# Attention and mixture kernel: values read once, POOL residues, a third turning bank and a new order

## The chip, the cores and the metric

The program runs on one core of a Trainium2 chip. The time is in device microseconds (us), the median of several executions of the whole program. The core's engines are TensorE (PE, with its weight load PEld), VectorE (DVE), ScalarE (ACT), GpSimd (POOL) and SyncE (SP). Each engine goes through its own instructions in a fixed order; semaphores hold an instruction back until what it needs is there. DMAs are issued from the queues of SP, ACT and POOL.

## The reference

Three layers, in float32, for 4 batches of 576 tokens. Attention with 8 heads of 64 and a decay; a gated mixture of 4 attention experts with top-2 routing; and a mixer: a low-rank mix over the sequence and a ReLU layer of 2048.

```python
scores = q @ k.T / 8 + cum[:, None] - cum[None, :]        # cum = cumsum(log(clip(f)))
x = softmax(where(causal, -1e9, scores)) @ v              # 8 heads -> x[B, 576, 512]
for e in range(4):                                        # mixture: q, k, v of x per expert
    ye = softmax(causal(x@wq[e] @ (x@wk[e]).T / 8)) @ (x@wv[e]) @ wo[e]
    out += gate_top2[e] * ye
u = out + (out.T @ U @ V).T                               # mixer; U, V, w_ch1, w_ch2 are float64
return u + maximum(u @ w_ch1, 0) @ w_ch2
```

## The kernel before

Most products are taken in pairs of float16: a number is scaled by a power of two, its rounded part `hi` is written by ACT and the rest, `lo = scale * x - hi`, by DVE (`split`); three products of hi and lo then give nearly float32. The scale comes from a largest or summed absolute value of the whole tile (`pow2`, with one small PE product `mm<-identr,cols` that spreads it over the partitions, and `scales`).

The work is written as generators ("threads"). A planner (`Plan`) runs them in simulated time: each thread says which engine it needs next, or which buffer of a ring (`Ring`) or event, and the planner picks the thread with the earliest time plus a penalty by its priority (`PR`, times `PEN`). The order in which it picks is the order in which the instructions stand on each engine. `LAG` is the time that it adds before a freed buffer may be taken again, and `BIAS` what it adds for an engine where a step may go to one of several (`Any`). None of these numbers stands in the program itself; they only move instructions and choose engines.

By batch the stages are these. Kind 1 is the attention of 8 heads: `scores` (PE, into the PSUM ring `sp`, 3 banks, or `acc`), `softmax` (DVE mask and maximum, ACT exp), the turning of the probabilities, and `pair_pv` with `pv_out` (the product with the values, in ring `mm`, 2 banks, and its division). `project` and `values_gates` form the experts' q, k, v and the gates. Kind 2 is the experts' attention, by the same functions. `mix` forms z; `hidden` (tiles `hid<-z,wfr`, ring `hid`, 1 bank) and `outputs` (tiles `acc<-w2x,g` and `acc<-wo,z`) are the last two layers, with `relu` between them. After `mix` of a batch its hidden and output products fill PE beside the heads of the next batch.

Probabilities are turned in one of two ways. For batch 0, and for the first two heads of batch 1, PE turns the float32 blocks (`turn_head`, line 628, `mm<-identr,sc`) and the split reads them from PSUM (`pt<-mm`). Elsewhere the split is taken first (tiles P, by `parts`: its second half on DVE or POOL) and a DMA turns P into pt.

Batch 0 carries extra work beside its heads: the weights w1 and w2 come as float64 and are turned to float32 (`f64_to_f32`: ACT, DVE and, for one product, POOL; tiles x, w2x, sg), w1 is folded with wo on PE (`fold`, ring `hid`, tiles `hid<-x,wtr`, into wfr), and wfr, w2x, wall, wo and U are split. `hidden` waits for all splits of wfr (`ev("wf")`) and for z.

`values` reads each batch's values v in four pieces of two heads (tile vr, 2 buffers, 320 KB each): once for the sum of the absolute values, and a second time, when the common scale SV is known, for the split into V (tiles V, 2 buffers of hi and of lo).

Of the kernel before, what the change touches and what calls it, by code (L numbers as in the profile page):

```python
# [20 lines left out]
KB = 5  # L21
# [3 lines left out]
EPS = 1e-9 * 2.0 ** 14  # L25
BIAS = {'act': 100.0, 'dve': 900.0, 'pool': 0.0}
XN = 1
# [13 lines left out]
WARM = 3300.0  # L41
LAG = 200.0
AHEAD = 16
PROJ_EXP = 15
PR = {'load': 4.25, 'low0': 1.25, 'low': 6.0, 'zeros': 1.75, 'scores': 1.5, 'soft0': 1, 'soft2_0': 2.0, 'soft': 6.5, 'soft2_': 6.5, 'pv0': -2.0, 'pv': 3.25, 'pvout0': 0, 'pvout': 3.25, 'project0': 3.5, 'project': 3.25, 'vg0': -1.25, 'vg': 4.25, 'out0': 1.0, 'out': 5.0, 'values0': 0.75, 'values': -0.75, 'wall': 4.5, 'prep': 5.0, 'f64': 0.5, 'f64_2': 2.25, 'fold': 1.75, 'wf': 0.5, 'w2': 6.25, 'mix': 0.0, 'relu': 1.5, 'store': -0.25, 'hidden': 4.5, 'outputs': 6}
TERMS = ((0, 0), (0, 1), (1, 0))

NEXT = (2, 0, 0, 0)
HEADS = [(1, 0, h) for h in range(8)]
ON_PE = lambda kind, b, h: b == 0 or (kind, b) == (1, 1) and h < NEXT[0]  # L50
for b_, n_ in enumerate(NEXT):
# [84 lines left out]


class Plan:
    GAP = {"pe": 0.0, "act": 130.0, "dve": 115.0, "pool": 130.0, "sp": 0.0}
# [49 lines left out]
    def run(self):  # L189
        while self.threads:  # L190
# [32 lines left out]
def attn_moe_mixer(ctx: ExitStack, tc: tile.TileContext, qk, v, f, wall, wot, wo, w1, w2, u3, v3, out):  # L223
# [213 lines left out]

    HY = {}
    HG, PT, VP, XT, SV, STG, GATE, YT, YN, IV, ZT, CS = {}, {}, {}, {}, {}, {}, {}, {}, {}, {}, {}, {}
# [106 lines left out]
    def softmax(key, blk, st, early, both):  # L546
# [5 lines left out]
        hold = key if blk else (kind, b, h // 2)  # L552
        on_pe = ON_PE(*key)
        if blk == 0 and on_pe:
# [58 lines left out]
    def turn_head(key):  # L613
# [5 lines left out]
        for c, blks, k0, k1 in ((0, (0, 1), 0, 5), (3, (2,), 0, 5), (6, (3,), 0, 5), (10, (4,), 0, 4), (14, (4,), 4, 5)):  # L619
            for blk in blks:  # L620
                yield ev("exp", key, blk)
            bank = yield r_mm
            i = 0
            for blk in blks:
                x = EXP[key, blk]
                yield "pe"
                for kb in range(k0, min(k1, blk + 1)):
                    nc.tensor.transpose(bank[:, 128 * i:128 * i + 128], x[:, 128 * kb:128 * kb + 128], identr)  # L628
                    plan.tensor(110, 128)
# [3 lines left out]

            def out_(bank=bank, c=c, i=i):
                hi, lo = (pt[:, 15 * t + c:15 * t + c + i, :].rearrange("k c q -> k (c q)") for t in range(2))
                yield from split(hi, lo, bank[:, :128 * i], 2.0 ** 14)
                r_mm.free(bank)
                n.done()
# [27 lines left out]
    def pair_pv(kind, b, p):  # L666
# [4 lines left out]
        else:  # L671
            yield ev("v2", b)
            vs, c0 = V2, 2 * p
        on_pe = ON_PE(kind, b, 2 * p)
        if not on_pe:
# [3 lines left out]
        for j in range(2):  # L679
# [33 lines left out]
    def pv_out(kind, b, p, j, bank, pv):  # L713
# [7 lines left out]
        yield "dve"  # L721
        ts(rr, pv[:, :, 64], EPS, ALU.add)
        recip(rr, rr)
# [39 lines left out]
    def values(b):  # L763
        if True:
            mx = col(f"mxv{b}", 4)
            for hp in range(4):
                vr = yield r_vr
                if hp == 2:
                    yield ev("rows of first")
                yield QUEUE[3]  # L770
                got = dma(vr, v[b][:, :, hp * 128:(hp + 1) * 128], queue(3))
                yield got
                yield "act"
                abssum(mx[:, hp:hp + 1], vr, vr)
                r_vr.free(vr)
            e = yield from pow2(f"v{b}", mx, 4)
            SV[b] = scales(f"v{b}", e, 14)
            for hp in range(4):
                vr = yield r_vr
                hi = yield r_vp[0]  # L780
                lo = yield r_vp[1]
                VP[b, hp] = (hi, lo)
                yield QUEUE[3]
# [3 lines left out]
                yield from split(hi[:, :, :, 0:64], lo[:, :, :, 0:64], x, SV[b][0])  # L787
                r_vr.free(vr)
                ev("vp", b, hp).done()
            if b + 1 < B:  # L790
                spawn(values(b + 1), PR['values'])

# [632 lines left out]
```

## Time and profile before

| | |
|---|---|
| median of 3 runs | 787.75 us (783.74 to 790.79) |
| the profiled execution: time, span | 790.84 us, 789.1 us |
| busy: PE, DVE, ACT, POOL | 667.4, 491.9, 425.9, 278.6 us |
| TensorE clock granted, mean | 0.942 |
| DMA | 110.64 MB, mean 140 GB/s |

The page and the views say for each engine how long it worked and what ended the idle time ahead of its instructions. Busy times of engines overlap, so they don't add up to the span. A granted clock of 1.00 is TensorE's 2.4 GHz, and 0.50 its lower level of 1.2 GHz; a stretch in between had both. In the rows, L241 is `mm`, L246 `act`, L252 `dve`, L264 `pool`, L270 and L272 the DMAs.

### The profile page before, as it was taken

The page shows a single profiled execution, that of the slowest core. Times are in us where ns is not written, and L with a number is a line of the kernel's source. Part 1 is how long each engine was busy: PE and PEld are TensorE (multiplying, and loading weights), DVE is VectorE, ACT ScalarE, POOL GpSimd, SP SyncE. Part 2 cuts the span into 40 slices and gives each one's busy share as a digit, 9 for nine tenths or more (in the row PEclk, how much of TensorE's full clock was granted, in tenths as well). Part 3 has the DMA queues.
Part 4 walks back from the last instruction along what each step waited for, and adds up shares of the span by engine and source line. Part 5 has one row for each costly group of instructions (what it writes and reads, how often), then busy time and mean ns, then how long its engine had stood idle before and what let it go on. Part 6 is the DMA issues. An engine that isn't in the chain of part 4 may idle for free.

```text
span 789.1 us, 15849 instructions
## 1 busy us (share of the span) xinstructions
PE 667.4 (85%) x5802; PEld 465.6 (59%) x5802; DVE 491.9 (62%) x1551; ACT 425.9 (54%) x891; POOL 278.6 (35%) x341
## 2 busy tenths in 40 slices
PE   2768897877578889898699898994999999899996
PEld 1456787655555557565466575663666756555553
DVE  4898797999979744775766366866663673311111
ACT  3777886787857643664557355654553562211121
POOL 4123235306745420477664114773751241000000
PEclk9999999977769999999799999996999999899999
DMA  8556545647899964999999549999985675000000
GB/s 232 162 133 178 158 128 155 202 116 180 173 179 153 149 152 100 184 193 228 210 187 181 107 120 184 183 211 203 184 145 93 121 133 80 27 0 27 1 27 27
DMA packets 213730, 110.64 MB, mean 140 GB/s; under 512 B 165012, under 2 KB 194708, under 8 KB 213620
## 3 DMA queue, kind: packets, MB, share of 16 engines
q1 hardware_dynamic: 182740, 79.37, 51.0%
q0 software_dynamic: 8096, 16.22, 10.7%
q10 hardware_dynamic: 22816, 14.03, 6.8%
q8 instruction: 46, 0.75, 0.4%
q14 instruction: 32, 0.26, 0.1%
HBM read 57.15 MB, written 5.16 MB: 79 GB/s over the span
## 4 chain that ended last, share of the span: by engine, by line
PE 33%; DMA 13%; DVE 9%; ACT 4%; issue 2%; POOL 1%; SPq 0%; ACTq 0%; DVEq 0%; POOLq 0%
PE acc L241 12%; PE mm L241 12%; DMA pt<-P 8%; PE hid L241 8%; DVE sc L252 2%; DVE P L252 2%; PE sp L241 2%; DMA R<-in_qk 2%; DMA PT<-P 1%; ACT P L246 1%; ACT sc L246 1%; DVE rr L252 1%; DMA wq<-lg 1%; DVE nm L252 1%; POOL P L264 1%
## 5 line engine op out<-in xcount | busy, mean ns | idle before, releaser
L241 PE MATMUL acc<-w2x,g 128*128 128x512 f16 x768 | 183.1, 384 | 0.4 <-DVE g L252 0.4
L264 POOL TENSOR_TENSOR P<-sc,P 128x320 f16<-128x320 f32 (+4 forms) x111 | 86.6, 787 | 171.1 <-ACT P L246 145.4
L241 PEld LDWEIGHTS <-g 128*128 128x128 f16 x864 | 82.5, 99 | 85.5 <-issue 3.0
L241 PE MATMUL hid<-z,wfr 128*128 128x256 f16 x864 | 115.6, 284 | 10.2 <-DVE g L252 5.9
L246 ACT ACTIVATE sc<-sc,nm 128x192 f32<-128x192 f32 (+4 forms) x185 | 99.8, 555 | 45.4 <-DVE nm L252 41.6
L252 DVE SCALAR_TENSOR_TENSOR g<-hid,g 128x512 f16<-128x512 f32 x72 | 49.5, 687 | 111.4 <-ACT g L246 111.1
L241 PEld LDWEIGHTS <-wfr 128*128 128x128 f16 x864 | 85.4, 102 | 36.6 <-issue 10.5
L246 ACT ACTIVATE g<-hid 128x512 f16<-128x512 f32 x72 | 42.5, 591 | 98.6 <-PE acc L241 62.0
L246 ACT ACTIVATE P<-sc 64x64 f16<-64x64 f32 (+4 forms) x163 | 69.4, 458 | 38.9 <-DMA pt<-P 35.7
L241 PE MATMUL mm<-V,pt 128*128 128x65 f16 x2058 | 76.3, 198 | 11.7 <-DMA pt<-P 5.3
L241 PEld LDWEIGHTS <-pt 128*128 128x128 f16 x2058 | 71.6, 101 | 14.9 <-issue 6.7
L241 PE MATMUL sp<-X 128*128 128x256 f32 (+1 forms) x132 | 51.9, 402 | 27.3 <-DVE nm L252 14.0
L252 DVE TENSOR_TENSOR P<-sc,P 128x576 f16<-128x576 f32 (+4 forms) x59 | 47.7, 811 | 35.7 <-ACT P L246 32.9
L264 POOL TENSOR_TENSOR xh<-xn,xh 128x320 f16<-128x320 f32 x30 | 26.8, 892 | 82.9 <-ACT xh L246 80.0
L628 PE MATMUL mm<-identr,sc 128*128 128x128 f32 x210 | 38.5, 302 | 17.8 <-DVE pt L252 12.4
L241 PEld LDWEIGHTS sp<-X 128*128 128x128 f32 x132 | 27.5, 208 | 40.0 <-DVE nm L252 20.4
L241 PE MATMUL mm<-xt,wall 128*128 128x288 f16 x384 | 49.6, 286 | 1.1 <-DVE stg L252 0.5
L252 DVE CUSTOM_DVE_ANT_0 sc<-sp,mask 64x64 f32<-64x64 f32 (+4 forms) x110 | 46.1, 424 | 6.5 <-PE sp L241 4.1
L264 POOL TENSOR_TENSOR x<-x,sg 128x512 f32<-128x512 f32 (+2 forms) x19 | 25.8, 1355 | 54.8 <-DVE x L252 42.8
L241 PEld LDWEIGHTS <-wall 128*128 128x128 f16 x384 | 37.5, 98 | 11.7 <-issue 1.9
L628 PEld LDWEIGHTS mm<-identr,sc 128*128 128x128 f32 x210 | 25.7, 151 | 31.6 <-DVE pt L252 15.0
L241 PE MATMUL sp<-Y 68*128 68x256 f32 (+1 forms) x132 | 42.4, 329 | 0.0
(142 smaller groups left out, 1194.8 us busy)
## 6 DMA issues: line engine op xcount, KB each, us to landing
wd<-in_w SPq DMA_DIRECT2D x32, 512.0 KB
vr<-in_v ACTq DMA_DIRECT2D x32, 320.0 KB
R<-in_qk SPq DMA_DIRECT2D x22, 288.0 KB
Y<-in_qk POOLq DMA_DIRECT2D x22, 288.0 KB, 4.7
X<-in_qk POOLq DMA_DIRECT2D x22, 288.0 KB, 5.6
out_dram<-o SPq DMA_DIRECT2D x18, 256.0 KB
Xh<-stg SPq DMA_DIRECT2D x16, 216.0 KB
X<-in_qk POOLq DMA_DIRECT2D x22, 144.0 KB, 4.7
```

What stands on the lines that cost most here:

```text
L241: nc.tensor.matmul(out_, lhsT=lhsT, rhs=rhs, start=start, stop=stop, **kw)
L246: nc.scalar.activation(out_, in_, fn, **kw)
L252: getattr(nc.vector, op)(**kw)
L264: getattr(nc.gpsimd, op)(out=out_, **kw)
L628: nc.tensor.transpose(bank[:, 128 * i:128 * i + 128], x[:, 128 * kb:128 * kb + 128], identr)
```

## The change

- `values` reads each piece once. Scales are taken by half a batch (two pieces): both pieces are loaded, summed (into a scratch tile `junk` from ring `xn`), scaled by their half's own scale and split from the same tile. When the second half's scale is known, a common scale SV is formed and a factor for each half (`RV`), which `pv_out` multiplies into the row sums. `pair_pv` of kind 1 waits for that (`ev("sv", b)`).
- `split` of a tile in SBUF may take its residue to POOL alone: two POOL operations (the scaling in place, then the subtraction) in place of one on DVE.
- `turn_head` of batch 0 takes a bank of `mm` or the bank of `hid`, whichever the planner has free earlier (`Either`).
- Which pairs PE turns stands in a table `TURN`. It names the same pairs as the expression before.
- `LAG` is 100 in place of 200, the bias of DVE 1000 in place of 900, and nearly all priorities `PR` are others.

```diff
-BIAS = {'act': 100.0, 'dve': 900.0, 'pool': 0.0}
+BIAS = {'act': 100.0, 'dve': 1000.0, 'pool': 0.0}
-LAG = 200.0
+LAG = 100.0
-PR = {'load': 4.25, 'low0': 1.25, 'low': 6.0, 'zeros': 1.75, 'scores': 1.5, 'soft0': 1, ...
+PR = {'load': 2.75, 'low0': -1.5, 'low': 6.0, 'zeros': -2.0, 'scores': 3.25, 'soft0': 1, ...
+TURN = {(1, 0): 4, (2, 0): 2, (1, 1): 1, (1, 2): 0}
+class Either:
+    def ready(self):
+        return any(r.ready() for r in self.rings)
+    def take(self, *a):
+        r = min((r for r in self.rings if r.ready()), key=lambda r: r.time())
+        return r, r.take(r.shape, r.dtype, r.name)
...
     def split(hi, lo, src, scale=1.0):
         yield "act"
         copy_scaled(hi, src, scale)
-        yield "dve"
-        residue(lo, src, hi, scale)
+        n = size(src)
+        if src.space == PSUM or (yield Any(dve=170 + 1.04 * n, pool=2 * (180 + 1.93 * n))) == "dve":
+            if src.space == PSUM:
+                yield "dve"
+            residue(lo, src, hi, scale)
+        else:
+            pool("tensor_scalar", src, in0=src, scalar1=scale, scalar2=None, op0=ALU.mult)
+            yield "pool"
+            pool("tensor_tensor", lo, in0=src, in1=hi, op=ALU.subtract)
...
-            bank = yield r_mm
+            r, bank = yield Either(*((r_mm, r_hid) if key[1] == 0 else (r_mm,)))
...
+            if kind == 1:
+                yield ev("sv", b)
...
-        ts(rr, pv[:, :, 64], EPS, ALU.add)
+        if kind == 1:
+            ts(rr, pv[:, :, 64], EPS, ALU.add, RV[b][p // 2], ALU.mult)
+        else:
+            ts(rr, pv[:, :, 64], EPS, ALU.add)
...
     def values(b):
...
+        for half in range(2):
+            for i in range(2):
                 vr = yield r_vr
...
+                got = dma(vr, v[b][:, :, hp * 128:(hp + 1) * 128], queue(3))
+            for i, (vr, got) in enumerate(vrs):
                 yield got
+                junk = yield r_xn.of([128, KB, 128], F16, "junk")
                 yield "act"
-                abssum(mx[:, hp:hp + 1], vr, vr)
-                r_vr.free(vr)
+                abssum(mx[:, i:i + 1], vr, junk)
+                r_xn.free(junk)
+            e = yield from pow2(f"v{b}{half}", mx, 2)
+            ss.append(scales(f"v{b}{half}", e, 14)[0])
+            if half == 1:
+                tt(e, es[0], es[1], ALU.max)
+                SV[b] = scales(f"v{b}", e, 14)
+                RV[b] = [times(f"rv{b}{i}", s, SV[b][1]) for i, s in enumerate(ss)]
+                ev("sv", b).done()
...
-                got = dma(vr, v[b][:, :, hp * 128:(hp + 1) * 128], queue(3))
-                yield got
...
+                yield from split(hi[:, :, :, 0:64], lo[:, :, :, 0:64], x, ss[half])
```

How the instructions then stand is shown at three places. Counted over the whole program, POOL takes over residues of two parts of wall and of two rows of wfr, and 16 P subtractions; DVE has 44 small instructions on `cols` more and 16 P subtractions fewer; ACT issues 16 reads of vr fewer; 95 of the 210 turning products go to the bank of `hid`.

**ACT at the program's start.** YW are the tiles of the first heads' q and k, aug the decay rows, vr the values, V their split. Before:

```order
L246 ACTIVATE vr,cols<-vr 128x640
L272 DMA vr<-in_v 128x5x128
L246 ACTIVATE vr,cols<-vr 128x640
L272 DMA YW_96<-aug 4x2x576
L272 DMA YW_94<-aug 4x2x576
L272 DMA vr<-in_v 128x5x128
L272 DMA YW_95<-in_qk 64x2x576
L272 DMA YW_95<-aug 4x2x576
L246 ACT_TABLE_LOAD
L246 ACTIVATE sc_97<-sp,nm 64x64
```

And now:

```order
L267 ACTIVATE junk,cols<-vr 128x640 x2
L293 DMA YW_96<-aug 4x2x576
L293 DMA YW_94<-aug 4x2x576
L267 ACTIVATE V_78<-vr,cols 128x10x64
L293 DMA YW_95<-in_qk 64x2x576
L293 DMA YW_95<-aug 4x2x576
L267 ACTIVATE V_79<-vr,cols 128x10x64
L267 ACT_TABLE_LOAD
L267 ACTIVATE sc_97<-sp,nm 64x64
L267 ACTIVATE sc_98<-sp,nm 128x192
L293 DMA vr<-in_v 128x5x128 x2
```

The first two pieces of the values are split ahead of the first exponential, and the third head's load now stands behind the first of these splits.

**PE at the first heads.** `sp` and `acc` are scores, `identr,sc` turned blocks, with the bank that they go to ahead of the arrow. Before:

```order
L241 MATMUL sp<-YW_96 128x64
L241 MATMUL sp<-YW_96 128x192
L241 MATMUL sp<-YW_96 128x320
L628 MATMUL mm<-identr,sc_97 128x128
L628 MATMUL mm<-identr,sc_98 128x128 x2
L241 MATMUL sp<-YW_96 128x448
L628 MATMUL mm<-identr,sc_99 128x128 x3
L241 MATMUL acc<-YW_96 128x288 x2
L241 MATMUL sp<-YW_94 128x64
L628 MATMUL mm<-identr,sc_100 128x128 x4
```

And now:

```order
L262 MATMUL sp<-YW_96 128x64
L262 MATMUL sp<-YW_96 128x192
L262 MATMUL sp<-YW_96 128x320
L262 MATMUL sp<-YW_96 128x448
L658 MATMUL hid<-identr,sc_97 128x128
L658 MATMUL hid<-identr,sc_98 128x128 x2
L262 MATMUL acc<-YW_96 128x288
L658 MATMUL mm<-identr,sc_99 128x128 x3
L262 MATMUL acc<-YW_96 128x288
L658 MATMUL mm<-identr,sc_100 128x128 x4
```

Turned blocks alternate over three banks, and a score product stands between them more often.

**POOL late in batch 0.** X, Y and R are the heads of batch 1 (X is the residue that their scores need), P the probabilities' residues, wfr the folded weights that `hidden` waits for. Before, with all eight residues of wfr on DVE, ahead of z:

```order
L264 TENSOR_TENSOR P_74<-sc_98,P_74 128x192
L272 DMA Y<-in_qk 64x2x576
L264 TENSOR_TENSOR X<-R,Y 64x576
L272 DMA X<-in_qk 64x2x576
L264 TENSOR_TENSOR X<-R,X 64x576
L264 TENSOR_TENSOR P_75<-sc_101,P_75 128x576
L272 DMA X<-in_qk 64x576
L264 TENSOR_TENSOR xh<-xn,xh 128x5x64
L264 TENSOR_TENSOR P_73<-sc_97,P_73 64x64
L264 TENSOR_TENSOR X<-R,Y 64x576
```

And now:

```order
L285 TENSOR_SCALAR wfr<-wfr,cols 128x512
L293 DMA Y<-in_qk 64x2x576
L285 TENSOR_TENSOR wfr<-wfr 128x512
L293 DMA X<-in_qk 64x2x576
L285 TENSOR_TENSOR P_75<-sc_100,P_75 128x448
L293 DMA X<-in_qk 64x576
L285 TENSOR_TENSOR P_75<-sc_101,P_75 128x576
L285 TENSOR_TENSOR X<-R,Y 64x576
L285 TENSOR_SCALAR wfr<-wfr,cols 128x512
L293 DMA Y<-in_qk 64x2x576
L285 TENSOR_TENSOR wfr<-wfr 128x512
```

The second residue of wfr on POOL now stands behind the residue X of the fourth head of batch 1 that is loaded this way, and on DVE four of the six that are left stand behind z's.

## Rows read from the trace of the kernel before

**Rows 1.** Busy time by stage: from:to, length, busy (instructions) by engine, PEclk, DMA share, GB/s.

```profile
20.00:232.00 212.00, 161.91 (x1531) 129.34 (x1530) 186.84 (x536) 160.60 (x343) 75.42 (x69) 0.91 0.65 162
232.00:276.00 44.00, 37.09 (x333) 25.44 (x331) 37.30 (x103) 30.52 (x61) 22.21 (x25) 0.95 0.93 143
276.00:680.00 404.00, 361.57 (x3333) 248.03 (x3332) 242.53 (x872) 210.13 (x448) 172.57 (x211) 0.95 0.85 158
680.00:789.20 109.20, 102.33 (x603) 59.64 (x601) 16.59 (x24) 18.34 (x30) 0.00 (x0) 0.97 0.04 15
```

**Rows 2.** DVE's waits, 20 to 232 us: total us, times, longest us.

```profile
DVE pt L252 <- ACT pt L246: 4.9, 8, 1.0
DVE rr L252 <- PE mm L241: 4.5, 7, 1.5
```

**Rows 3.** The chain that ended last, by engine.

```profile
PE 33%; DMA 13%; DVE 9%; ACT 4%; issue 2%; POOL 1%; SPq 0%; ACTq 0%; DVEq 0%; POOLq 0%
```

**Rows 4.** PE's waits, 232 to 680 us.

```profile
PE mm L241 <- DMA PT<-P: 8.6, 3, 3.4
...
PE sp L241 <- POOL X L264: 5.1, 1, 5.1
```

**Rows 5.** The chain in order of time, where the tail begins.

```profile
677.99 9.52 PE hid L241 x59
```

**Rows 6.** DVE in order of time: start, us, what, idle before.

```profile
17.08 0.24 DVE L252 CUSTOM_DVE_ANT_0 sp<-sp,mask 64x64 f32<-64x64 f32 x1 [6.36 <-PE sp L241]
```

**Rows 7.** DVE's groups by shape, 0 to 276 us: busy us, mean ns.

```profile
L252 DVE SCALAR_TENSOR_TENSOR V<-vr,cols,V 128x640 f16<-128x640 f32 x8 | 8.4, 1049 | 0.7 <-ACT V L246 0.6
...
L252 DVE SCALAR_TENSOR_TENSOR wfr<-wfr,cols 128x512 f16<-128x512 f32 x8 | 6.0, 747 | 0.0
...
L252 DVE SCALAR_TENSOR_TENSOR wall<-w2x,cols,wall 128x1024 f16<-128x1024 f32 x3 | 4.8, 1584 | 0.0
...
L252 DVE TENSOR_TENSOR cols<-cols 128x1 f32<-128x1 f32 x11 | 3.6, 330 | 0.3
...
L252 DVE TENSOR_SCALAR cols<-cols 128x1 f32<-128x1 f32 x24 | 3.6, 151 | 0.7
...
L252 DVE TENSOR_TENSOR P<-sc,P 128x320 f16<-128x320 f32 x5 | 2.8, 550 | 0.0
...
L252 DVE TENSOR_TENSOR P<-sc,P 128x448 f16<-128x448 f32 x2 | 1.9, 936 | 0.0
```

**Rows 8.** PE's waits, 0 to 232 us.

```profile
PE mm L628 <- DVE pt L252: 12.4, 15, 2.3
```

**Rows 9.** DMA on the page: all bytes, and two kinds of issues.

```profile
DMA packets 213730, 110.64 MB, mean 140 GB/s; under 512 B 165012, under 2 KB 194708, under 8 KB 213620
...
vr<-in_v ACTq DMA_DIRECT2D x32, 320.0 KB
...
Y<-in_qk POOLq DMA_DIRECT2D x22, 288.0 KB, 4.7
```

**Rows 10.** POOL's group of the float64 products, 0 to 290 us.

```profile
L264 POOL TENSOR_TENSOR x<-x,sg 128x512 f32<-128x512 f32 x16 | 23.0, 1436 | 29.7 <-DVE x L252 17.6 <-PE mm L628 5.8 <-ACT sc L246 3.2
```

**Rows 11.** POOL and DVE in order of time, 249 to 258.6 us.

```profile
251.37 1.40 POOL L264 TENSOR_TENSOR X<-R,X 64x576 fp32r<-64x576 f32 x1
251.41 1.92 DVE L252 SCALAR_TENSOR_TENSOR w2x<-w2x,cols 128x512 f16<-128x512 f32 x1
...
254.11 0.75 DVE L252 SCALAR_TENSOR_TENSOR w2x<-w2x,cols 128x512 f16<-128x512 f32 x1 [0.32 <-ACT w2x L246]
```

**Rows 12.** The hidden stage's start, in order of time, 228 to 240 us.

```profile
232.26 1.38 PE L241 MATMUL hid<-z,wfr 128*128 128x256 f16 x6
...
236.00 1.40 POOL L264 TENSOR_TENSOR X<-R,Y 64x576 fp32r<-64x576 f32 x1
```

**Rows 13.** The next such residue of X on POOL.

```profile
248.80 1.39 POOL L264 TENSOR_TENSOR X<-R,Y 64x576 fp32r<-64x576 f32 x1 [0.90 <-DMA R<-in_qk]
```

**Rows 14.** Busy time, 220 to 240 us.

```profile
220.00:240.00 20.00, 17.10 (x129) 12.32 (x129) 16.42 (x52) 11.85 (x22) 11.11 (x12) 0.66 0.87 167
```

More of the change, by code (lines that the diff above doesn't have):

```diff
@@ L41 @@
 WARM = 3300.0
-LAG = 200.0
+LAG = 100.0
 AHEAD = 16
 PROJ_EXP = 15
-PR = {'load': 4.25, 'low0': 1.25, 'low': 6.0, 'zeros': 1.75, 'scores': 1.5, 'soft0': 1, 'soft2_0': 2.0, 'soft': 6.5, 'soft2_': 6.5, 'pv0': -2.0, 'pv': 3.25, 'pvout0': 0, 'pvout': 3.25, 'project0': 3.5, 'project': 3.25, 'vg0': -1.25, 'vg': 4.25, 'out0': 1.0, 'out': 5.0, 'values0': 0.75, 'values': -0.75, 'wall': 4.5, 'prep': 5.0, 'f64': 0.5, 'f64_2': 2.25, 'fold': 1.75, 'wf': 0.5, 'w2': 6.25, 'mix': 0.0, 'relu': 1.5, 'store': -0.25, 'hidden': 4.5, 'outputs': 6}
+PR = {'load': 2.75, 'low0': -1.5, 'low': 6.0, 'zeros': -2.0, 'scores': 3.25, 'soft0': 1, 'soft2_0': 1.0, 'soft': 5.5, 'soft2_': 7.0, 'pv0': -1.0, 'pv': 1.75, 'pvout0': 2.0, 'pvout': 4.75, 'project0': 3.75, 'project': 2.25, 'vg0': 0.75, 'vg': 4.75, 'out0': 1.0, 'out': 3.0, 'values0': 1.0, 'values': -1.0, 'wall': 5.25, 'prep': 6.5, 'f64': -1.25, 'f64_2': 3.25, 'fold': 2.25, 'wf': 1.75, 'w2': 3.75, 'mix': 0.25, 'relu': 0.0, 'store': 2.75, 'hidden': 6.25, 'outputs': 8.25}
 TERMS = ((0, 0), (0, 1), (1, 0))
+TURN = {(1, 0): 4, (2, 0): 2, (1, 1): 1, (1, 2): 0}
 NEXT = (2, 0, 0, 0)
 HEADS = [(1, 0, h) for h in range(8)]
-ON_PE = lambda kind, b, h: b == 0 or (kind, b) == (1, 1) and h < NEXT[0]
 for b_, n_ in enumerate(NEXT):
@@ L135, in free, with __init__, of, time @@
             self.over.done(self.end[id(t)])
+class Either:
+    def __init__(self, *rings):
+        self.rings = rings
+    def of(self, shape, dtype, name):
+        return self, shape, dtype, name
+    def ready(self):
+        return any(r.ready() for r in self.rings)
+    def time(self):
+        return min(r.time() for r in self.rings if r.ready())
+    def take(self, *a):
+        r = min((r for r in self.rings if r.ready()), key=lambda r: r.time())
+        return r, r.take(r.shape, r.dtype, r.name)
 class Plan:
@@ L552, in softmax @@
         hold = key if blk else (kind, b, h // 2)
-        on_pe = ON_PE(*key)
+        on_pe = key[2] // 2 < TURN.get(key[:2], 0)
         if blk == 0 and on_pe:
@@ L632, in turn_head, with out_ @@
                     r_sc[blk].free(EXP.pop((key, blk)))
-            def out_(bank=bank, c=c, i=i):
+            def out_(r=r, bank=bank, flat=flat, c=c, i=i):
                 hi, lo = (pt[:, 15 * t + c:15 * t + c + i, :].rearrange("k c q -> k (c q)") for t in range(2))
-                yield from split(hi, lo, bank[:, :128 * i], 2.0 ** 14)
-                r_mm.free(bank)
+                yield from split(hi, lo, flat[:, :128 * i], 2.0 ** 14)
+                r.free(bank)
                 n.done()
@@ L673, in pair_pv @@
             vs, c0 = V2, 2 * p
-        on_pe = ON_PE(kind, b, 2 * p)
+        on_pe = p < TURN.get((kind, b), 0)
         if not on_pe:
@@ L763, in values @@
     def values(b):
-        if True:
-            mx = col(f"mxv{b}", 4)
-            for hp in range(4):
+        es, ss, last = [], [], []
+        for half in range(2):
+            mx = col(f"mxv{b}{half}", 2)
+            vrs = []
+            for i in range(2):
                 vr = yield r_vr
-                if hp == 2:
+                if half == 1 and b == 0:
                     yield ev("rows of first")
                 yield QUEUE[3]
+                hp = 2 * half + i
                 got = dma(vr, v[b][:, :, hp * 128:(hp + 1) * 128], queue(3))
+                vrs.append((vr, got))
+            for i, (vr, got) in enumerate(vrs):
                 yield got
+                junk = yield r_xn.of([128, KB, 128], F16, "junk")
                 yield "act"
-                abssum(mx[:, hp:hp + 1], vr, vr)
-                r_vr.free(vr)
[L776 to L779, printed above, removed]
+                abssum(mx[:, i:i + 1], vr, junk)
+                r_xn.free(junk)
+            e = yield from pow2(f"v{b}{half}", mx, 2)
+            es.append(e)
+            ss.append(scales(f"v{b}{half}", e, 14)[0])
+            if half == 1:
+                yield "dve"
+                e = col(f"ev{b}")
+                tt(e, es[0], es[1], ALU.max)
+                SV[b] = scales(f"v{b}", e, 14)
+                RV[b] = [times(f"rv{b}{i}", s, SV[b][1]) for i, s in enumerate(ss)]
+                ev("sv", b).done()
+            for i, (vr, got) in enumerate(vrs):
+                hp = 2 * half + i
                 hi = yield r_vp[0]
```

13 lines of the change are left out of this document (6 added, 7 removed).

## The prediction

> **What bounds the kernel now.** I read the busy time by stage first [rows 1], because the shares over the whole span mix three regimes. From 20 to 232 us, batch 0 with the weights' preparation, DVE works 186.84 of 212 us and ACT 160.60, while PE has 161.91 at a mean granted clock of 0.91: here DVE sets the pace, ACT close behind. From 232 to 276 us DVE still has 37.30 of 44 us: it splits w2 while hidden and output products begin. From 276 to 680 us PE has 361.57 of 404 us and DVE only 242.53: PE is the bound, with bubbles. From 680 us on PE works without a pause; the chain in order of time shows that stretch beginning with hidden products at 677.99 us [rows 5], three groups of the last batch that need its z. So the time is the moment of the last z plus a fixed tail, and an edit pays by making DVE's part shorter or PE's bubbles fewer.
>
> Next the waits. DVE is idle 25.16 us between 20 and 232 us, and the largest named parts are 4.9 us for ACT's half of the turned blocks' splits and 4.5 us for PE's value products [rows 2]. In the chain of work that ended last, DMA has 13% and POOL 1% [rows 3]. Between 232 and 680 us PE waited 8.6 us for one kind of turning DMA and once, 5.1 us, for the residue X from POOL [rows 4].
>
> **The start.** DVE's first score operation comes after 6.36 us of idleness [rows 6]. The order now puts two V residues of 1.049 us [rows 7] and their scale chain there; ACT's two splits stand there too. They leave the DVE-bound stretch, which takes 2 us off (0 to 2: nothing, if the scale chain comes late and pushes the first scores back instead).
>
> **DVE's work up to the last residue of w2** (276 us). Counting the order up to that instruction and pricing by shape [rows 7]: gone are one wall part (1.584), two wfr rows (2 x 0.747), four P residues of 320 and one smaller at that price (5 x 0.550), two of 448 (2 x 0.936): 7.70 us. New are 11 scalar operations on `cols` and as many reduces and reciprocals, all at 0.151 (3.32), six `cols` products at 0.330 (1.98) and one V residue that has moved ahead (1.049): 6.35 us. The rest pairs off. Net 1.4 us, say 1.5 off (0 to 3). That is little: the change takes fewer residues from DVE than it sounds, because only wall and wfr pass to POOL, none of V or w2, and half-batch scales add small operations of the fixed price.
>
> **The third bank.** PE waited 12.4 us, 15 times, for DVE to empty a turned bank [rows 8]. PE isn't the bound there, so this is not the gain; the gain is what ACT and DVE get back when the next block already lies in PSUM. That can't be more than the 4.9 + 4.5 us of DVE's waits [rows 2], and it can be nothing, since folds also use the `hid` bank and then queue with the blocks. Between 0 and 9.4 I take 4 off, nearer the 4.9 that the blocks' splits alone show.
>
> **The reads.** 16 reads of 320 KB go, 5.2 of 110.64 MB [rows 9], 4.7%. If DMA's 13% of the chain [rows 3], 103 us, shrank in proportion, it would be 4.8 us; the reads in batch 0 relieve nothing that the chain waits for. I take 3 off (0 to 6). The wait for the second half's scale is costed at nothing: behind it on PE stand the pair's products, but in the order the sums of batch 1 stand ahead of its first value product by most of batch 0, and the later ones by a whole expert stage. Were that cover gone, each batch would pay about a load's 4.7 us (a 288 KB one [rows 9]), and the next stage would be late by that.
>
> **POOL.** It gets eight operations for wall and wfr and 16 P residues; a 128x512 one takes 1.436 us [rows 10]. Batch 0 leaves POOL 137 us idle between 20 and 232 us [rows 1], so its own time is covered. But it is not free for DVE: a w2 residue that begins 0.04 us after a POOL operation on two SBUF tiles takes 1.92 us, and 0.75 alone [rows 11], 1.17 more. If half of the eight meet such a DVE operation, that is 4.7 us; some P residues have left DVE and can't be hit any more. I take 1.5 on, bounds 0 and 9 (all eight).
>
> The Trainium skill says it more strictly ("SBUF — State Buffer", section "Who interferes with whom"): a DVE instruction with two SBUF inputs and a GpSimd one that reads SBUF exclude each other, and the later one blocks fully. By that rule, as an estimate, all eight operations could be paid in full, 8 x 1.17 = 9.4 us, and the sum below would come to about nothing; the rows of the w2 residues agree with the rule as far as they go.
>
> **Where hidden begins.** This is where the order gives something back. Before, the wfr residues were done long before z, and hidden began at 232.26 us [rows 12]. Now four of DVE's wfr residues, three of w2 and that of wo stand behind z's, and POOL's second wfr residue behind the fourth X. In the trace that X starts at 236.00 us [rows 12]; with its 1.40 us and two operations of 1.4, wfr would be complete at 240 us at the old pace, 5 to 7 us earlier at the new one. PE has other products meanwhile (value products and scores of batch 1 and the wo products, some 8 us that used to stand behind the first hidden products). So it begins some us later but with that much more done: I count zero (4 either way).
>
> **Later batches.** PE's order from batch 1 on is the same to within a few products, so PE's bubbles should stay, less what DMA gives. The table `TURN` names the same pairs as before: zero.
>
> **The sum.** -2 - 1.5 - 4 - 3 + 1.5 + 0 = -9 us. Against the profiled execution's 790.84 us that is 781.8; against the median of the runs, 3.1 us lower at 787.75, it is 778.8, so 779.
>
> **Rivals.**
>
> *The bank does more (768).* If turned blocks never hold ACT and DVE back, most of the 25.16 idle us [rows 1] goes, not only the two named waits: 15 us in place of 4, so -20. For it: the waits are many and short, the mark of a shallow queue. Against it: z's own chain of maxima lies in that idleness too.
>
> *The gain is paid back (785).* DVE and POOL meet more often than I count, and the P residues on POOL, longer in the queue, hold back turning DMAs in later batches; +6 on the forecast. Its mark is that the two-SBUF residues lengthen. The skill's rule in the page named above is the strict form of this; by rows it is the 1.92 against 0.75.
>
> *Hidden begins a step late (797, the slower side).* The X residues come at a pace of their own, set by heads' loads and buffers: 236.00, then 248.80 us [rows 12, 13]. If the second wfr residue on POOL slips by one such step, hidden begins 12.8 us later than forecast, PE runs dry after its 8 us of other products, and the granted clock falls as it did from 220 to 240 us, where 17.10 us of PE work at 0.66 are 11.3 at full clock [rows 14], 5.8 us. 779 + 12.8 + 5.8 = 797.6. It decides when wfr is complete later than about 243 us. For it: POOL executes in order, and a longer queue stands ahead. Against it: POOL was idle for almost half of 220 to 240 us.
>
> *It does not do what it says:* if the planner's new numbers only shuffle the order, nothing but the reads is left, 785 or more; this goes with the second rival.
>
> **How the numbers follow.** About 1% is what a measurement of this kernel can tell from no change; the runs before lie 0.9% apart. Forecast, 772 to 787 us: 0.45, of which somewhat more than half lies below 779.9. The bank does more: 0.13. Paid back or nothing changed, 784 to 790: 0.22. A step late: 0.20. So faster by over 1%: 0.28 + 0.13 = 0.41; slower by over 1%: 0.19, since the last rival just passes 795.6; within 1%: 0.40. The favourable bounds together, -2 - 3 - 9.4 - 6, give 767; the slower rival gives 797 and a little more if POOL's blocking joins it. Range 766 to 799.
>
> **What would show it.** Right: the first hidden product at 234 to 240 us; DVE idle between 20 us and that moment at most 20 us; V residues ahead of or among the first scores at 10 to 18 us; the moment of the last z at 667 to 672 us; the tail still 111 us; 105.4 MB moved. Wrong: hidden at 245 us or later with PE idle ahead of it (a step late); wait of PE for X or P longer than 5.1 us, or residues of 1.4 us and more in number (paid back); PE bubbles in batches 1 to 3 that changed by more than 5 us, which my count of the order would have missed.

## The result, and the profile after

The changed kernel takes **780.99 us** (median of 20 runs, 775.48 to 792.37) against 788.29 us (20 runs, 779.98 to 796.89): ratio 0.9915, 95% interval 0.9885 to 0.9944, which makes 6.7 us less. Ratios, here and below, leave out of each kernel the slow executions, those over 1.5% above its fastest, while medians are of all. Forecast were 779 us and -9. The profiled execution took 780.9 us, its span 779.2, 9.9 less than before; the one profiled before had taken 790.84 us, 2.6 above that kernel's median, so the spans overstate the gain by some 3 us.

Busy time by stage of the changed kernel, as in [rows 1]:

```profile
20.00:232.00 212.00, 165.30 (x1536) 131.42 (x1536) 178.77 (x532) 155.20 (x338) 86.72 (x79) 0.89 0.61 151
232.00:276.00 44.00, 34.92 (x284) 22.64 (x283) 40.41 (x103) 33.54 (x64) 28.46 (x30) 0.81 0.69 135
276.00:680.00 404.00, 373.20 (x3436) 257.42 (x3437) 242.42 (x890) 213.21 (x455) 177.80 (x219) 0.97 0.84 152
680.00:779.20 99.20, 92.42 (x541) 52.74 (x539) 15.21 (x22) 17.15 (x28) 0.00 (x0) 0.98 0.05 17
```

Against [rows 1], DVE is 8.07 us less busy from 20 to 232 us, and PE 11.63 us busier from 276 to 680 us. Where a batch stands is best read from its z residue on DVE, the operation for which the batch's hidden products wait. Its start in the trace, in us, with the first hidden product and the span (kernels of the experiments below are listed with them):

| kernel | z of batch 0 | 1 | 2 | 3 | first hidden | span |
|---|---|---|---|---|---|---|
| before | 229.4 | 388.0 | 547.2 | 676.5 | 232.3 | 789.1 |
| after | 232.2 | 383.5 | 537.5 | 667.9 | 250.3 | 779.2 |
| after2 | 229.7 | 385.4 | 548.2 | 677.2 | 247.4 | 788.5 |
| again | 235.2 | 388.2 | 546.0 | 676.0 | 252.8 | 787.0 |
| again_tiny | 233.4 | 384.0 | 540.7 | 669.8 | 251.0 | 781.1 |
| again_sp | 230.7 | 384.8 | 543.6 | 674.6 | 248.4 | 786.0 |
| tiny64 | 246.1 | 406.3 | 571.7 | 703.4 | 266.6 | 814.8 |
| sp48 | 238.2 | 393.6 | 559.7 | 693.4 | 255.8 | 806.0 |
| v_sp | 233.2 | 383.7 | 536.1 | 664.7 | 249.7 | 776.0 |
| resdve | 234.2 | 385.7 | 539.5 | 669.6 | 250.4 | 779.3 |

So batch 0 **lost** 2.8 us. From z to z, batch 1 gained 7.3 us (158.6 to 151.3) and batch 2 5.2 (159.2 to 154.0); batch 3 lost 1.1, and from the last z to the end there are 1.3 less (112.6 to 111.3). That is +2.8 - 7.3 - 5.2 + 1.1 - 1.3 = -9.9. The gain is where the prediction put nothing but the reads, and batch 0 gave none of the 6 us that its other terms had promised.

One execution stands behind each row. `after2` is the changed kernel once more in the same order (an execution of 790.24 us), and `v_sp` and `resdve` differ from it little. Over these four rows z of batch 0 comes at 229.7 to 234.2 us, batch 1 takes 150.5 to 155.7 us and batch 2 152.4 to 162.8. That batch 0 gained nothing and batch 1 gained stands in each of them; the 5.2 us of batch 2 don't, and differences of a few us between two rows are within what one kernel shows by itself.

**Batch 0.** DVE in order of time, after:

```profile
13.40 0.89 DVE L273 SCALAR_TENSOR_TENSOR V<-vr,cols,V 128x640 f16<-128x640 f32 x1 [0.90 <-ACT V L267]
15.70 0.24 DVE L273 CUSTOM_DVE_ANT_0 sp<-sp,mask 64x64 f32<-64x64 f32 x1 [1.40 <-PE sp L262]
...
16.71 0.88 DVE L273 SCALAR_TENSOR_TENSOR V<-vr,cols,V 128x640 f16<-128x640 f32 x1
```

Two V residues lie among the first scores, which begin 1.4 us earlier than in [rows 6]: the start went as drawn. What followed did not. Busy time of two later stretches of batch 0, before:

```profile
100.00:180.00 80.00, 65.75 (x612) 54.45 (x611) 73.25 (x193) 62.26 (x131) 26.41 (x20) 0.93 0.52 146
180.00:240.00 60.00, 40.32 (x356) 30.61 (x354) 52.08 (x153) 42.55 (x93) 36.21 (x39) 0.75 0.88 178
```

and after:

```profile
100.00:180.00 80.00, 71.38 (x712) 58.88 (x710) 60.61 (x183) 57.88 (x128) 27.68 (x27) 0.98 0.60 164
180.00:240.00 60.00, 34.86 (x285) 28.21 (x285) 55.08 (x149) 45.76 (x100) 47.40 (x46) 0.65 0.89 190
```

From 100 to 180 us DVE fell from 73.25 of 80 us to 60.61, while PE rose to 71.38: there DVE no longer sets the pace. From 180 to 240 us PE has only 34.86 of 60 at a clock of 0.65, and DVE 55.08. The relief came early, and the work that had been put off met z at the end of the batch. Over 20 to 232 us DVE's idle time went from 25.16 to 33.23 us.

**The third bank.** PE's waits from 0 to 232 us, after:

```profile
PE hid L658 <- DVE pt L273: 10.9, 8, 3.2
...
PE mm L658 <- DVE pt L273: 1.9, 4, 1.1
```

[rows 8] had 12.4 us, all on the old banks; now it is 10.9 + 1.9 = 12.8, most of it in front of the new one. DVE's two waits of [rows 2], after:

```profile
DVE pt L273 <- ACT pt L267: 4.3, 9, 1.1
...
DVE rr L273 <- PE mm L262: 2.9, 4, 1.2
```

7.2 us in place of 9.4. ACT's waits for turned blocks (`pt`) add up to 10.1 us, before 14.1.

**Where hidden begins.** The end of the wfr chain in order of time, after, on DVE, POOL and PE:

```profile
232.24 1.74 DVE L273 SCALAR_TENSOR_TENSOR z<-y,cols,z 128x1152 f16<-128x1152 f32 x1
...
241.09 0.74 DVE L273 SCALAR_TENSOR_TENSOR wfr<-wfr,cols 128x512 f16<-128x512 f32 x1
...
246.78 1.91 DVE L273 SCALAR_TENSOR_TENSOR wfr<-wfr,cols 128x512 f16<-128x512 f32 x1
```

```profile
234.27 1.17 POOL L285 TENSOR_TENSOR wfr<-wfr 128x512 f16<-128x512 f32 x1
```

```profile
250.27 2.78 PE L262 MATMUL hid<-z,wfr 128*128 128x256 f16 x12
```

POOL was done at 235.4 us and DVE's last wfr residue, which begins 14.5 us after z, at 248.7. PE's order puts two score products of the next batch right ahead of the hidden ones, and those waited longer:

```profile
249.41 0.69 PE L262 MATMUL sp<-X 128*128 128x448 f32 x1 [2.33 <-DVE nm L273]
```

The maximum `nm` that released them stands behind that wfr residue on DVE. So the first hidden product comes 18.0 us later than in [rows 12], by DVE's order and not by POOL's. The rival's event came true: wfr complete later than 243 us, PE idle and its clock down. Busy time of the stretch, before:

```profile
232.00:250.00 18.00, 16.49 (x140) 10.90 (x138) 17.20 (x52) 13.64 (x27) 10.96 (x13) 0.96 0.70 150
```

and after:

```profile
232.00:250.00 18.00, 10.29 (x69) 6.19 (x68) 17.56 (x41) 12.05 (x21) 11.22 (x12) 0.61 0.70 142
```

Its price didn't come. Up to their first hidden products PE had been busy 166.7 us before and 182.5 after, from the union of its instructions in the trace. At the mean granted clocks up to there (0.91 and 0.88) that is, as an estimate, 152 and 161 us at full clock: some 9 us more work in 18.0 us.

**DMA.** All bytes and the loads of values on the page after, for [rows 9]:

```profile
DMA packets 203234, 105.40 MB, mean 135 GB/s; under 512 B 164756, under 2 KB 184212, under 8 KB 203124
...
vr<-in_v ACTq DMA_DIRECT2D x16, 320.0 KB
```

PE's waits from 232 to 680 us, for [rows 4]:

```profile
PE sp L262 <- POOL X L285: 6.1, 3, 2.5
...
PE mm L262 <- DMA PT<-P: 0.7, 1, 0.7
```

The wait for turned P of the last rows fell from 8.6 to 0.7 us, all waits of PE's for turned P from 13.9 to 4.1. ACT waits too: before it writes the next P, it waits until a turning transfer has read the last one. That wait over the whole span, before:

```profile
ACT P L246 <- DMA pt<-P: 35.7, 24, 4.6
```

and after:

```profile
ACT P L267 <- DMA pt<-P: 21.5, 17, 4.8
```

14.2 us less, and 33.1 of the 35.7 us lay behind 232 us, in the batches whose P is turned by DMA. That wait by itself is no measure of the time: it is 24.2 us in `after2`, 25.1 in `resdve` and 26.3 in `v_sp`, whose span is the shortest of all.

### The profile page after: what moved, and what is told of

It is laid out like the page before. It is cut to its first block, busy times and chain, and to the rows that moved or that the text cites. A ratio compares the mean times of both kernels' runs of the same rounds, so it can differ in the third digit from the quotient of the medians.

```text
span 779.2 us, 15886 instructions
## 1 busy us (share of the span) xinstructions
PE 672.5 (86%) x5810; PEld 468.7 (60%) x5810; DVE 488.5 (63%) x1573; ACT 426.4 (55%) x894; POOL 302.0 (39%) x364
## 5 line engine op out<-in xcount | busy, mean ns | idle before, releaser
L262 PE MATMUL acc<-w2x,g 128*128 128x512 f16 x768 | 180.2, 380 | 0.5 <-ACT g L267 0.4
L285 POOL TENSOR_TENSOR P<-sc,P 64x64 f16<-64x64 f32 (+4 forms) x127 | 98.2, 779 | 139.4 <-ACT P L267 108.8
L267 ACT ACTIVATE sc<-sc,nm 128x576 f32<-128x576 f32 (+4 forms) x185 | 100.3, 555 | 45.4 <-DVE nm L273 39.1
L267 ACT ACTIVATE P<-sc 128x448 f16<-128x448 f32 (+4 forms) x167 | 71.7, 458 | 23.3 <-DMA pt<-P 21.5
L262 PE MATMUL sp<-X 128*128 128x256 f32 (+1 forms) x132 | 53.7, 416 | 23.7 <-DVE nm L273 13.9
L273 DVE TENSOR_TENSOR P<-sc,P 128x576 f16<-128x576 f32 (+4 forms) x43 | 36.4, 847 | 30.8 <-ACT P L267 30.4
L273 DVE CUSTOM_DVE_ANT_0 sc<-sp,mask 128x448 f32<-128x448 f32 (+4 forms) x110 | 46.3, 425 | 9.5 <-POOL P L285 3.9
L285 POOL TENSOR_TENSOR xh<-xn,xh 128x320 f16<-128x320 f32 x29 | 26.3, 908 | 66.9 <-ACT xh L267 56.8
L285 POOL TENSOR_TENSOR x<-x,sg 128x512 f32<-128x512 f32 (+2 forms) x18 | 23.1, 1286 | 65.8 <-DVE x L273 52.2
L273 DVE CUSTOM_DVE_ANT_0 sc<-sp,mask,cols 128x320 f32<-128x320 f32 (+4 forms) x75 | 35.8, 486 | 7.2 <-POOL P L285 3.8
L285 POOL TENSOR_TENSOR X<-R,Y 64x576 fp32r<-64x576 f32 x22 | 32.3, 1468 | 15.4 <-DMA R<-in_qk 15.2
```

The lines of the kernel that those rows point to most:

```text
L262: nc.tensor.matmul(out_, lhsT=lhsT, rhs=rhs, start=start, stop=stop, **kw)
L267: nc.scalar.activation(out_, in_, fn, **kw)
L273: getattr(nc.vector, op)(**kw)
L285: getattr(nc.gpsimd, op)(out=out_, **kw)
```

## The experiments

Theory R (reads): the 16 reads less are the gain. Its two forms are **traffic** (their bytes in the way of the turning transfers) and **issue** (ACT's time to issue them). Rivals: the third bank, POOL's share of the residues, and the order that the planner's numbers give. In `again`, `again_tiny`, `again_sp`, `tiny64`, `sp48`, `v_sp` and `resdve` everything but the lines shown stands in the changed kernel's order. Ratios are to the kernel before, with 95% intervals.

**again: the 16 reads are put back,** into a DRAM tensor that nobody uses, ahead of each V split.

```diff
+    again = dram.tile([16, 128, KB, 128], F32, name="again")
...
+    nc.scalar.dma_start(out=again[4 * b + hp], in_=v[b][:, :, hp * 128:(hp + 1) * 128])
```

> The changed kernel with every instruction in the same order, and 16 DMAs more on ACT's queue: at each split of a piece of the values the same 320 KB are read once more, into a scratch in DRAM that nobody reads. Theory 'reads' (the 9 us came in batches 1 to 3 because 16 reads less let the turning DMAs land earlier): 5 to 9 us slower than the changed kernel, PE's waits for turning DMAs between 232 and 680 us back from 4.1 to 10 us or more, the z of the third batch 5 us later. Theory 'order' (the later batches gained because the new priorities place turns and products differently): within 2 us of the changed kernel, waits for turning DMAs under 7 us.

786.3 us, ratio 0.9999 [0.9966, 1.0031]: all of the gain is gone; `resdve`, which ran beside it without the reads, has 0.9923. ACT's wait for turning transfers, again:

```profile
ACT P L267 <- DMA pt<-P: 33.7, 20, 5.0
```

It is nearly back at its 35.7 us. PE's own waits for turned P, from 232 to 680 us, are not:

```profile
PE mm L262 <- DMA PT<-P: 2.4, 2, 2.0
...
PE mm L262 <- DMA pt<-P: 2.1, 3, 1.0
```

Expected were 10 us or more, and 4.5 came, against 4.1 in the changed kernel: that part of PE's waits went with the new order, not with the reads. By the table 8.1 us are lost up to the last z: 3.0 in batch 0, 1.7 in batch 1, 3.8 in batch 2, and 0.4 won in batch 3. The 3.0 I put down to the place. ACT in order of time in this kernel:

```profile
13.16 0.83 ACT L267 ACTIVATE V<-vr,cols 128x640 f16<-128x640 f32 x1 [2.84 <-DMA YW<-aug]
...
13.96 0.50 ACTq L293 DMA_DIRECT2D YW<-aug  x1
19.26 0.54 ACTq L835 DMA_DIRECT2D again<-in_v  x1
19.85 0.83 ACT L267 ACTIVATE V<-vr,cols 128x640 f16<-128x640 f32 x1 [5.87 <-DMA YW<-aug]
```

The second extra issue began 4.80 us after the one ahead of it had ended, and the split behind it 6.08 us later than in the changed kernel (13.77 us there). In the trace that issue waits for a semaphore that the first extra read counts up, and the last of its 16 counts came at 19.24 us: it was held until the first extra read had landed. The kernel before had its V residues of batch 0 from 44 us on, well behind these first issues. So by this trace the reads themselves are worth the 5.1 us of batches 1 to 3, and `again` overstates them by some 3. Behind the first z stand nine of the 16 (four, four and one between one z and the next), which is why batch 3 shows nothing.

**resdve: POOL's residues of wall and wfr go back to DVE.**

```diff
-            pool("tensor_scalar", src, in0=src, scalar1=scale, scalar2=None, op0=ALU.mult)
...
-            pool("tensor_tensor", lo, in0=src, in1=hi, op=ALU.subtract)
+            nc.vector.scalar_tensor_tensor(out=lo, in0=src, scalar=scale, in1=hi, op0=ALU.mult, op1=ALU.subtract)
```

> The changed kernel with PE, ACT and SP in the same order; the four residues of wall and wfr that POOL took with two operations each are single operations on DVE again, at the place in DVE's order where the planner has them. If POOL's residues help DVE: hidden products begin 2 to 4 us later than 250.5 us and the time is 1 to 4 us longer. If POOL's eight operations blocked DVE as much as they spared it: the same moment and the same time within 2 us. If POOL held hidden back: hidden begins earlier than 248 us.

780.42 us, ratio 0.9923 [0.9892, 0.9954], the changed kernel's 0.9915 again. Busy time in it:

```profile
20.00:232.00 212.00, 166.82 (x1533) 132.27 (x1533) 179.47 (x529) 153.85 (x335) 74.33 (x72) 0.88 0.60 151
```

POOL is 12.39 us less busy and DVE only 0.70 more than in the changed kernel, though residues of 2.25 us came back to DVE in this stretch; z of batch 0 begins 2.0 us later without a trace of it in the time. The part as a whole, what POOL takes over and what it blocks, neither helps nor hurts measurably; the two sides aren't priced apart.

**breads: the kernel before with the reads once alone,** its own planner numbers, the order planned anew; beside the lines shown it has the changed kernel's values(b) and its wait for the common scale.

```diff
-        ts(rr, pv[:, :, 64], EPS, ALU.add)
+        if kind == 1:
+            ts(rr, pv[:, :, 64], EPS, ALU.add, RV[b][p // 2], ALU.mult)
+        else:
+            ts(rr, pv[:, :, 64], EPS, ALU.add)
```

> The kernel before with one part of the change alone: each piece of the values read once, scales by half a batch, the wait for the common scale and the factor in the row sums. The planner's numbers are those of before; the order follows anew. Theory 'reads': 5 to 9 us faster than the kernel before, PE's waits for turning DMAs between 232 and 680 us down from 13.9 to about 5 us. Theory 'order': within 3 us of the kernel before, either way, waits for turning DMAs still above 9 us.

818.39 us, 1.0387 [1.0334, 1.044]: the slowest of all. Its order is another, with z of batch 0 only at 257.3 us, so it doesn't price the reads; what it stands for comes with the next three.

**wf_early: wfr is planned earlier,** to bring hidden back to z.

```diff
-PR = {..., 'wf': 1.75, ...}
+PR = {..., 'wf': -3.0, ...}
```

> The changed kernel with the priority of the thread that scales and splits wfr raised (PR of wf from 1.75 to -3), so that all of wfr's residues stand ahead of z's of batch 0 or just behind it; folds as late as they were. If the late start of hidden (250.5 us in the changed kernel, 232.3 before) costs time: hidden begins at 236 to 244 us and the time is 4 to 8 us shorter than the changed kernel's. If PE fills that stretch with other work anyway and DVE's sum sets the pace: hidden begins earlier but the last residue of w2 stays at 279 us, and the time is within 2 us.

801.9 us, 1.0221 [1.0168, 1.0275]. Hidden began at 234.4 us, as before, and z of batch 0 at 233.6, but z of batch 1 came at 397.1, 13.6 us later than in the changed kernel. Busy time in this kernel:

```profile
340.00:400.00 60.00, 47.53 (x425) 32.10 (x424) 36.20 (x136) 32.90 (x69) 39.90 (x47) 0.87 1.12 200
```

PE has 47.53 of 60 us there, ahead of that z, and 52.38 in the changed kernel. An early hidden stage didn't help this order: the moment to which batch 1 leads is its z, and it was reached later. What the early stage is worth by itself it doesn't show, since the whole order is another.

**twobank: the changed kernel without the third bank,** and **oldnum: with the numbers of the kernel before** (the table `PR` too); both planned anew.

```diff
-            r, bank = yield Either(*((r_mm, r_hid) if key[1] == 0 else (r_mm,)))
+            r, bank = yield Either(r_mm)
```

```diff
-BIAS = {'act': 100.0, 'dve': 1000.0, 'pool': 0.0}
+BIAS = {'act': 100.0, 'dve': 900.0, 'pool': 0.0}
...
-LAG = 100.0
+LAG = 200.0
```

> The changed kernel with turned blocks of batch 0 in the two banks of mm alone, as before; the numbers of the planner are those of the changed kernel, the order follows anew. Theory 'bank' (the third bank is worth the 4 us of the forecast): 2 to 8 us slower than the changed kernel, DVE's and ACT's waits around turned blocks longer, z of batch 0 later. Theory 'no bank': the bank is worth nothing by itself; the time differs only by what the new order does, and DVE's waits for ACT's half of the turned splits stay at 4 to 5 us.

> The changed kernel with the planner's numbers of before (priorities, LAG, bias of DVE), all code of the change kept. If the code of the change carries the gain: within 4 us of the changed kernel. If the order must fit the code, as the run with the single reads on the old numbers (3.9% over the kernel before) and the one with an earlier wfr (2.2% over) suggest: 10 us or more slower than the changed kernel, with the z of batch 0 later than 245 us.

790.89 us, 1.0078 [1.0033, 1.0124], and 790.65 us, 1.0084 [1.004, 1.0129]; the spans of their profiled runs were 794.2 and 788.2. Both have z of batch 0 late, at 249.8 and 247.9 us. Without the bank DVE's wait for the blocks' splits didn't grow:

```profile
DVE pt L273 <- ACT pt L267: 2.7, 7, 0.9
```

so it isn't that wait which costs twobank its time. ACT's waits for turned blocks are 14.6 us, in the changed kernel 10.1 and before 14.1, but the order is another too. That is what these four runs say together: whoever takes out or puts in one part and plans anew gets another order, here 0.8 to 3.9% slower than the kernel before, and the numbers belong to the code for which they were found. No such run prices its part.

**again_tiny and again_sp: issue and traffic apart.** 16 transfers of 512 bytes from ACT, and 16 of 320 KB from SP.

```diff
+    nc.scalar.dma_start(out=again[4 * b + hp][0:1, 0:1], in_=v[b][0:1, 0:1, hp * 128:(hp + 1) * 128])
```

```diff
+    nc.sync.dma_start(out=again[4 * b + hp], in_=v[b][:, :, hp * 128:(hp + 1) * 128])
```

> The changed kernel, same order on every engine, with 16 DMAs of 512 bytes more on ACT's queue, at the places where the run with the repeated reads had its 320 KB ones. That run lost the whole gain. Theory 'issue' (a read costs because ACT's sequencer spends 0.55 us on issuing it, 16 x 0.55 = 8.8 us): 5 to 8 us slower than the changed kernel. Theory 'traffic' (it costs because its bytes delay the turning DMAs of P, which ACT waits for before it writes the next P): within 2 us of the changed kernel, ACT's wait for those DMAs stays near 21.5 us.

> The changed kernel, same order on every engine, with the 16 repeated reads of 320 KB issued from SP's queue in place of ACT's. Theory 'issue': within 2 us of the changed kernel, or a little more where SP's queue stands still behind a wait. Theory 'traffic': 5 to 8 us slower than the changed kernel, ACT's wait for the turning DMAs of P back to about 34 us.

783.22 us, 0.9969 [0.9935, 1.0002], and 782.77 us, 0.9989 [0.9948, 1.003]. Both lie between the changed kernel and `again`, and their intervals overlap each other: either half may bring back part of the time. In the table the tiny ones cost 1.9 us up to the last z, the bytes 6.7 (8.2 of it in batches 1 to 3); but the profile of again_sp is of the longest of its twelve executions, 787.71 us, 4.9 above their median. ACT's waits for turning transfers are 27.4 us with the tiny ones, where the traffic theory had them stay near 21.5, and 28.9 with the bytes, where it had them back at 34.

**tiny64, sp48, after2, v_sp: the same, amplified.** Four tiny issues on ACT, or three reads from SP, in the place of each removed read; the changed kernel itself for comparison; and the 12 loads of values of batches 1 to 3 issued by SP.

```diff
...
+    for t_ in range(4):
+        nc.scalar.dma_start(out=again[4 * b + hp][0:1, 0:1, 32 * t_:32 * t_ + 32], in_=v[b][0:1, 0:1, hp * 128 + 32 * t_:hp * 128 + 32 * t_ + 32])
```

```diff
...
+    for t_ in range(3):
+        nc.sync.dma_start(out=again[3 * (4 * b + hp) + t_], in_=v[b][:, :, hp * 128:(hp + 1) * 128])
```

```diff
...
-    got = dma(vr, v[b][:, :, hp * 128:(hp + 1) * 128], queue(3))
+    got = dma(vr, v[b][:, :, hp * 128:(hp + 1) * 128], queue(3), by=nc.sync if b else None)
```

> The changed kernel once more, so that the other kernels of this group are compared with it on the same chip. All theories: the ratio that it had, 0.9915 (0.988 to 0.995), about 781 us. If it comes out above 0.997 the gain itself is in doubt, and the earlier split between issues and traffic with it.

> The changed kernel, order of PE, DVE, POOL and SP unchanged, with 64 transfers of 128 bytes issued by ACT, four in the place of each removed read: next to no bytes, four times the issues. Issue theory: the removed reads were paid in ACT's time, 0.55 us each (16 tiny ones gave 2 to 4 us), so 64 give 8 to 16 us more than the changed kernel in the same group, at most 35 if every one lay on the path. Traffic theory: nothing, within 2 us of it. Both in part: 4 to 8 us.

> The changed kernel, order of PE, DVE, ACT and POOL unchanged, with 48 reads of 320 KB issued by SP, three in the place of each removed read: 15.7 MB more, and no issue on ACT. Traffic theory: 16 of them gave 2 to 6 us, so 48 give 6 to 18 us more than the changed kernel in the same group, and ACT's wait for the turning transfers of P rises above the 29 us that it had with 16. Issue theory: nothing, within 2 us, or a few us where SP's own turning transfers queue behind three issues.

> The changed kernel with the 12 loads of values of batches 1 to 3 issued by SP in place of ACT, the order of everything else unchanged. Issue theory: ACT is spared 12 x 0.55 = 6.6 us, of which 1 to 3 us show in the time. Traffic theory: nothing. Against both: SP works in order, and a load that stands behind a turning transfer which still waits for its data comes late, and V's residues and the first value products of the batch with it: 0 to 5 us more.

After2: 781.0 us, 0.9955 [0.9918, 0.9993]; the gain repeats, smaller. Tiny64: 811.44 us, 1.0346 [1.0279, 1.0413], 30.4 us above after2. Sp48: 806.89 us, 1.0252 [1.0181, 1.0324], 25.9 above. V_sp: 785.26 us, 0.9966 [0.991, 1.0022], no change. So **amplified, both forms cost time**, each more than the 8 to 16 and 6 to 18 us that were expected (tiny64 less than the 35 of issues that all lie on the path). Of sp48's 25.5 us up to the last z, batch 2 has 12.1. Its busy time from 276 us on, with the DMA share at 0.92 against 0.84 and PE's 361.12 us near the 361.57 of [rows 1]:

```profile
276.00:680.00 404.00, 361.12 (x3370) 248.90 (x3369) 243.50 (x877) 212.95 (x453) 182.44 (x224) 0.96 0.92 170
```

and its wait of ACT:

```profile
ACT P L267 <- DMA pt<-P: 35.0, 21, 7.3
```

Three issues in a row on SP also stand in front of turning transfers, so not all of it need be bytes. Tiny64 has its own surprise at the start, ACT in order of time:

```profile
12.50 2.50 ACTq L836 DMA_DIRECT2D again<-in_v  x4
...
17.99 6.95 ACTq L836 DMA_DIRECT2D again<-in_v  x4
24.99 0.83 ACT L267 ACTIVATE V<-vr,cols 128x640 f16<-128x640 f32 x1 [9.11 <-DMA again<-in_v]
```

The second four took 6.95 us: the third of them, like the held one in `again`, waited for an earlier load (YW<-in_qk) to land. Batch 0 ended 13.9 us late; batches 1 and 2 lost 8.9 and 11.4 us, close to the 16 x 0.60 = 9.6 us that the 16 issues between two z's take at their median. Issues in a row are paid nearly in full. Single ones may cost little, since 12 of them moved from ACT to SP (v_sp) gave nothing that can be measured. For the change itself the split between 16 issues and 5.2 MB stays open. By the ratios the tiny ones cost 4 us and the bytes 6 over the changed kernel's 0.9915, and 1 and 3 over the 0.9955 of after2; the profiles that give the bytes the larger share rest on again_sp's longest execution. None of the versions beats the changed kernel.

## Why the prediction was right, and where by luck

The size was right (-9 forecast, -6.7 measured, -9.9 by the spans), the place was not. By its steps:

- **The start, -2.** V residues stand at 13 and 17 us, as foreseen, and the first score came 1.4 us earlier. Nothing of it reached z. The step that failed, for this term and the next two, is "DVE sets the pace in batch 0": shares of 20 to 232 us hid that DVE could be relieved from 100 to 180 us and be late from 180 us on.
- **DVE's work, -1.5.** The busy time fell more than that (8.07 us in the stage), in part because four wfr residues and z itself now stand behind 232 us; the folds, for which wfr waits, ended at 199.7 us, before at 140.3. Its idle time grew by as much, as it must in a stretch of fixed length. A sum of instructions up to a moment is worth nothing if the order leaves the engine waiting.
- **The third bank, -4.** PE's wait for turned banks is the same (12.4, now 12.8), DVE's two waits are 2.2 us shorter and ACT's for turned blocks 4.0; z of batch 0 was no earlier for it. The mark that I gave, idle DVE of at most 20 us before hidden, failed: it is 33.23 already by 232 us. The bank by itself wasn't priced by any run.
- **POOL, +1.5.** `resdve` gives zero for blocking and relief together. Contention is there (the wfr residue of 1.91 us above against 0.74, beside an X on POOL at 246.74 us), but what it costs alone isn't shown. The time gives no sign of the rival that is paid in such blocking; of its marks, PE's wait for X came by the letter, 6.1 us against 5.1.
- **The reads, -3.** Probably too small. They are worth 5.1 us in batches 1 to 3 by the trace of `again`, and with them back the time is that of before, 0.8% or 6 us above `resdve` beside it. The price had been taken from DMA's share of the chain, which doesn't show the turning transfers' wait on ACT, 35.7 us.
- **Where hidden begins, 0.** Its working failed. Forecast were 234 to 240 us and 250.27 came, since only POOL's last residue was timed, and DVE's four behind z were not. The prediction's own mark of a step late came with it, hidden after 245 us and PE idle ahead of it, at a clock of 0.61. PE had some 9 us more work done by then, near the 8 that were allowed, so half of the 18.0 us was not filled. It isn't to be seen in the next z all the same, which came 4.5 us earlier than before; whether the zero holds, no run shows.
- **Later batches, 0 beside the reads.** Wrong by this pair of profiles: batches 1 and 2 gained 12.5 us, of which the reads explain some 5. The prediction named bubbles changed by over 5 us as its own mark of a miscount. One thing that the order did itself is shown: PE's waits for turned P fell by 9.8 us and stayed low with the reads back. PE's work done ahead of a late hidden stage is another plausible source, since batch 1 then starts with less to do. How much of the remaining 7 us either made, no run isolates, and the spans overstate the whole gain by some 3.
- **The tail.** Forecast were 111 us from the last batch's first hidden product on. The chain in order of time, after, has that moment:

```profile
669.34 8.26 PE hid L262 x59
```

That leaves 779.2 - 669.34 = 109.9 us, and the last z, at 667.9 us, lies in the 667 to 672 us that were given for it.

In sum: -6 forecast for batch 0 came out as +2.8, -3 for the rest as -12.7, and the errors cancelled each other: the size was right by luck.

## What to carry to other kernels

When transfers are taken away, look for the engine that may not overwrite its source until a transfer has read it; a DMA share of the chain misses that. Such a wait names the place and not the price: ACT's was 21.5 to 26.3 us in kernels that read alike. When a planner sets the order, price parts with the order frozen and suspects added back, and then amplified; planning anew with a part removed measures the order. A stage's bound engine is to be read in slices: relieving it where another engine already paces the work moved the queue here to the stage's end. One profile is one execution: before a gain is split by batch, profile the same kernel twice.

## What the runs showed of the hardware

An issue on ACT's queue took 0.55 us for 320 KB as for 512 bytes (medians 552 and 555 ns of 16). But an issue can be held: two loads of values take 4.24 us in the changed kernel itself, and four of 128 bytes 6.95 us, though no single one of the 64 took over 1.39. ACT, in order of time, after:

```profile
16.90 4.24 ACTq L293 DMA_DIRECT2D vr<-in_v  x2
21.19 1.05 ACT L267 ACTIVATE sc<-sp,nm 128x320 f32<-128x320 f32 x2 [3.94 <-DMA YW<-in_qk]
```

The trace shows what held it. The first of the two takes 0.57 us, the second 0.56, and 3.05 us lie between them: the second waits for a semaphore that YW<-in_qk, a load of 288 KB issued at 12.54 us on the same queue, counts up, and the last of its 16 counts comes at 20.50 us, 0.03 us ahead of the issue's going on. In tiny64 the last count comes at 23.69 us and the held issue begins at 23.71. So the hold is a wait for an earlier load of the queue to land, and whatever ACT has behind it waits too. Later in the program four tiny issues took 2.43 to 3.53 us. In the kernel before such waits ahead of ACT's issues come to 0.7 us in all, so the removed reads weren't paid by them.
